# One guard over two columns becomes two guards over one, and a column total moves back in TensorE's order

## The chip, the cores and the metric

One NeuronCore of a Trainium2 chip runs the kernel as one program. The metric is the device time of an execution in microseconds; the time of a kernel is the median of its runs.

## What is computed

An attention layer with pooled keys is followed by two feed-forward layers. For 12288 tokens of 128 channels:

```python
kv_pool = kv.reshape(B, H // r, r, W // r, r, C).mean(axis=(2, 4))   # r = 4, 768 keys
k = v = kv_pool.reshape(B, -1, C) @ w_sr
s = (1.0 / np.sqrt(C)) * (q @ k.transpose(0, 2, 1))
a = np.exp(s - s.max(-1, keepdims=True))
a /= a.sum(-1, keepdims=True) + 1e-09
x = a @ v
h = x @ w_in                                       # 128 -> 2048
x = (np.maximum(h, 0) + alpha * np.minimum(h, 0)) @ w_out
h = x @ w_in2
x = (h * (1.0 / (1.0 + np.exp(-1.702 * h)))) @ w_out2
```

## The kernel before

The tokens go in 24 blocks `j` of 512 columns; channels lie on the 128 partitions. Every float32 operand of a large product is split into a high and a low float16 part, and a product is three matmuls (L443, L444, L445: high by high, low by high, high by low), which are 128x512 each. A block has four tiles of scores (`S`, L692 to L696), six products with the values (`V`), and 16 products in each of the four layers `L1` to `L4`.

Before a split the operand is scaled by a power of two, so that it fits float16. The scale comes from a bound on the largest absolute value. VectorE takes the maximum of each partition (`top`, L612, L764, L766) into `ta`; the **guard**, a `tensor_scalar` with max (it has the line of the helper `ts`, L408), lifts it to at least 2^-60 and writes it as bfloat16 to `td`; TensorE adds up the partitions with a matrix of ones, the **total** (`total`, name `scmm`, L622); VectorE takes the exponent out of the sum (`scp`) and turns it into the factor (`scc`). Then ScalarE writes the high part (L640) and VectorE the low one (L642). Three operands of a block are scaled so: `q`, `x` (the attention's output) and `y` (the output of the first feed-forward layer).

`x_prep(j)` for `j` from 3 to 21 does x of block `j` and q of block `j + 2` together: two maxima stand in the two columns of `ta2`, one guard over both columns writes `td2`, one total has two columns. `scale_of` is the way of all the others, with one column; it has the guard from block 3 on (`j > 2`).

A total, and every product of `L1` and `L3`, writes one of the three PSUM banks of `pool_h` (in the profile two of them are `hb` and one is `bk`). ScalarE and VectorE empty a bank: L830 (relu) and L832 (prelu) behind `L1`, L871 (tanh) and L873 (gelu) behind `L3`. The float16 parts of the hidden layers are made by ScalarE (L808) and, by a subtraction, mostly by GpSimd (L811).

The order of the instructions of each engine is worked out when the program is built. `op` records an operation with its engine, the time for which it keeps the engine, its duration, what it reads and writes, and a priority. `Plan.order` then places them one by one: the first 725 by the hand-made list `ORDER`, all later ones by taking for each engine what can start first in the plan, and among equals the lowest priority. An operation may start when what it reads has ended, plus a latency from `LAT` (54 ns from VectorE to TensorE); an entry of the read list may carry a third member, an offset that is taken off that time. TensorE is one queue in order: what waits at its head holds up everything behind it.

Of the kernel before, what the change touches and what calls it, by code (L numbers as in the profile page):

```python
# [17 lines left out]
ALU = mybir.AluOpType  # L18
# [98 lines left out]
class Plan:  # L117
# [5 lines left out]
    def op(self, eng, occ, dur, fn, r=(), w=(), prio=0.0, gate=None, name="", lock=False, dma=False):  # L123
        o = Op()
        o.eng, o.occ, o.dur, o.fn, o.gate, o.name, o.lock, o.dma = eng, occ, dur, fn, gate, name, lock or eng == "POOL", dma or eng == "SP"
        o.keys = [k for k in (self.tag, name.split(",")[0] if name.startswith(LAYER) else name) if k]
        o.prio = prio + sum(SHIFT.get(k, 0) for k in o.keys)
        k = f"{self.tag}|{name}"
        self.seen[k] = self.seen.get(k, -1) + 1
        o.uid = f"{k}|{self.seen[k]}"  # L130
        o.warm = 0
        o.n, o.succs, o.start, o.end = len(self.ops), [], None, None
        preds = {}

        def need(p, off):
            if p is not o:
                preds[p] = min(preds.get(p, off), off)

        bufs = []
        for x in r:  # L140
            b, part, off = (x + (0,))[:3] if isinstance(x, tuple) else (x, None, 0)
            if part not in b.writers:
                raise RuntimeError(f"{name} reads {b.name} {part} before it is written")
            for p in b.writers[part]:
                need(p, off)
            b.readers.setdefault(part, []).append(o)
            bufs.append(b)
        for x in w:
            b, part = x[:2] if isinstance(x, tuple) else (x, None)
            for p in b.readers.get(part, ()):  # L150
                need(p, 0)
            for p in b.writers.get(part, ()):
                need(p, 0)
            if (b, part) not in [(y[0], y[1]) if isinstance(y, tuple) else (y, None) for y in r]:
                b.readers[part] = []
            b.writers[part] = [o]
            bufs.append(b)
        o.bufs = list(dict.fromkeys(bufs + [b.also for b in bufs if b.also]))
        for b in o.bufs:
            b.ops.append(o)  # L160
        if gate is not None:
            preds.setdefault(gate, None)
        o.preds = list(preds.items())
        self.ops.append(o)
        return o
# [202 lines left out]
def dve(ns, n):  # L368
    return int(ns - 1.04 * (TB - n))
# [14 lines left out]
def record(nc, T):  # L384

    pl = Plan()
    op = pl.op
# [6 lines left out]
    def cols(ap, j):  # L394
        return ap[:, 0:SZ[j]]
# [7 lines left out]
    def fixed(name):  # L403
        return Buf(None, name)

    def ts(out, in0, s1, op0, s2=None, op1=None):
        if op1 is None:
            return V.tensor_scalar(out=out, in0=in0, scalar1=s1, scalar2=None, op0=op0)  # L408
        else:
            return V.tensor_scalar(out=out, in0=in0, scalar1=s1, scalar2=s2, op0=op0, op1=op1)  # L410

    def small(fn, r, w, prio, gate=None, occ=66, dur=150, name="small", lock=False):
        return op("DVE", occ, dur, fn, r, w, prio, gate, name, lock)
# [6 lines left out]
    pool_h = Pool([Slot(None, [cell[2]]), Slot(None, [cell[3]]), Slot(single[0], [cell[4]])])  # L420
# [15 lines left out]
    def new(name):  # L436
        return rings[name].buf(name)

    B = {name: fixed(name) for name in ("ident", "ones", "wsr", "al", "oma", "k_hi", "k_lo", "v_hi", "v_lo", "vsc", "vun", "kq",
                                        "kx", "kxc", "ky", "kyc", "kk", "vm", "wh", "wl", "am", "aov", "warm")}  # L440
# [169 lines left out]
    def top_of(j, x, xb, psum, prio, gate):  # L610
        d = new("td" if j < 3 else "ta")
        op("DVE", dve(608 if psum else 593, SZ[j]), dve(692, SZ[j]), lambda: V.tensor_reduce(out=d.ap, in_=x(), axis=AX.X, op=ALU.max,  # L612
                                                                     apply_absolute_value=True), [xb], [d], prio, gate, name="top")
        return d

    def total(pool, cols_, least, prio, n=1):

        pm = pool.buf("pt")

        def f():  # L620
            for i, (c, _) in enumerate(cols_):
                mm(out=pm.ap[:, 0:n], lhsT=T["ones"], rhs=c(), start=i == 0, stop=least is None and i == len(cols_) - 1)  # L622
            if least is not None:
                mm(out=pm.ap[:, 0:n], lhsT=T["ones"], rhs=least, start=False, stop=True)
        op("PE", 45 * len(cols_) + (45 if least is not None else 0), 0, f, [b for _, b in cols_] + [B["ones"]], [pm], prio, name="scmm")
        return pm

    def scale_of(d, pool, kc, kcb, prio, j=0):
        if j > 2:
            a, d = d, new("td")  # L630
            small(lambda: ts(d.ap, a.ap, 2.0 ** -60, ALU.max), [a], [d], prio)
        pm = total(pool, [(lambda: d.ap, d)], None if j > 2 else T["least"], prio)
        p, c = new("scp"), new("scc")
        small(lambda: ts(p.ap, pm.ap[:, 0:1].bitcast(I32), 0x7F800000, ALU.bitwise_and), [pm], [p], prio, occ=117)
        small(lambda: ts(c.ap, p.ap, -1.0, ALU.mult, kc(), ALU.add), [p] + kcb, [c], prio + .01, occ=110, dur=200)
        return c, p

    def parts(j, hi, lo, x, xb, c, prio, gate=None, psum=True):
        n = SZ[j]
        op("ACT", act(569 if psum else 613, n), act(700 if psum else 742, n), lambda: A.activation(cols(hi.ap, j), x(), AF.Copy, scale=c.ap.bitcast(F32)),  # L640
           [xb, c], [hi], prio, gate, name="hi")
        op("DVE", dve(665, n), dve(750, n), lambda: V.scalar_tensor_tensor(out=cols(lo.ap, j), in0=x(), scalar=c.ap.bitcast(F32), in1=cols(hi.ap, j),  # L642
                                                           op0=ALU.mult, op1=ALU.subtract), [xb, c, hi], [lo], prio + .01, gate, name="lo", lock=not psum)
# [115 lines left out]
    def x_prep(j, prio):  # L759
        x = xacc[j]  # L760
        pl.tag = f"X{j}"
        if 2 < j < NB - 2:
            t, a, d, p2, c, qc_ = q_t[j + 2], new("ta2"), new("td2"), new("scp2"), new("scc"), new("qcc")
            op("DVE", dve(593, TB), dve(692, TB), lambda: V.tensor_reduce(out=a.ap[:, 1:2], in_=t.ap, axis=AX.X, op=ALU.max, apply_absolute_value=True),  # L764
               [t], [(a, 1)], prio, name="top")
            op("DVE", dve(608, TB), dve(692, TB), lambda: V.tensor_reduce(out=a.ap[:, 0:1], in_=x.ap, axis=AX.X, op=ALU.max, apply_absolute_value=True),  # L766
               [x], [(a, 0)], prio, name="top")
            small(lambda: ts(d.ap, a.ap, 2.0 ** -60, ALU.max), [(a, 0), (a, 1)], [d], prio + .01)
            pm = total(pool_h, [(lambda: d.ap, d)], None, prio + .1, 2)
            small(lambda: ts(p2.ap, pm.ap[:, 0:2].bitcast(I32), 0x7F800000, ALU.bitwise_and), [pm], [p2], prio + .1, occ=117)  # L770
            p, q = Half(p2, 0), Half(p2, 1)
            small(lambda: ts(c.ap, p.ap, -1.0, ALU.mult, T["kxc"], ALU.add), [p2, B["kxc"]], [c], prio + .11, occ=110, dur=200)
            small(lambda: ts(qc_.ap, q.ap, -1.0, ALU.mult, QC, ALU.add), [p2], [qc_], prio + .12)
            qc[j + 2] = qc_, q
        else:
            d = top_of(j, lambda: cols(x.ap, j), x, True, prio, None)
            c, p = scale_of(d, pool_h, lambda: T["kxc"], [B["kxc"]], prio + .1, j)
        xh[j], xl[j] = new("xh"), new("xl")
        parts(j, xh[j], xl[j], lambda: cols(x.ap, j), x, c, prio + .2)
        xsc[j] = p  # L780
        pl.tag = ""
# [111 lines left out]

    q_prep(0, -660)
    vp = total(pool_x, [(lambda i=i: T["vm"][:, i:i + 1], (B["vm"], i)) for i in range(3)], T["least_v"], -650)
    small(lambda: ts(T["vun"], vp.ap[:, 0:1].bitcast(I32), 0x7F800000, ALU.bitwise_and), [vp], [B["vun"]], -647, occ=117)
    small(lambda: ts(T["vsc"], T["vun"], -1.0, ALU.mult, float(268 << 23), ALU.add), [B["vun"]], [B["vsc"]], -646)
# [30 lines left out]
    for t in range(SZ[0] // P):  # L928
        att_v(0, t, PR["v0"] + PR["a0s"] * t, None)
    x_prep(0, PR["x0"])  # L930

    for n, x in enumerate(LOADS):
# [183 lines left out]
```

## Time and profile before

| | us |
|---|---|
| median of 3 runs | 1259.17 |
| lowest and highest | 1256.1, 1259.45 |
| the profiled execution | 1257.87 |
| its span, first to last instruction | 1255.8 |
| TensorE busy in the span | 1215.5 |
| a block in the steady part, from total to total (1017.59 to 1067.77) | 50.18 |

The profile is of one execution. A matmul is shown with a duration of 0.38 us, but the next one of the same engine starts earlier; the rate at which TensorE works is read from the distance of the starts. The granted clock of TensorE is full throughout (1.000 in the mean).

### The profile page before, as it was taken

What the parts mean: (1) busy time and instruction counts of PE and PEld (TensorE: products, weight loads), DVE (VectorE), ACT (ScalarE), POOL (GpSimd) and SP (SyncE); (2) the same over time, 40 slices, a digit from 0 to 9 for tenths busy, and PEclk for the clock granted to TensorE, in tenths of its full rate; (3) what the DMA queues carried; (4) which work ended last, traced back from release to release, by engine and by line L of the source; (5) the groups of instructions that cost most, each with busy time, mean ns of one, the idle gap of its engine ahead of it and who ended that gap; (6) DMA issues with size and microseconds to landing.
All of it is one profiled execution on the core that took longest, in us unless ns stands there. A gap on an engine that the chain in (4) does not pass through costs nothing.

```text
span 1255.8 us, 18308 instructions
## 1 busy us (share of the span) xinstructions
PE 1215.5 (97%) x5829; PEld 569.3 (45%) x5832; DVE 1005.0 (80%) x1821; ACT 1099.7 (88%) x1939; POOL 804.8 (64%) x688
## 2 busy tenths in 40 slices
PE   5699999999999999999999999999999999999998
PEld 4344444444444444444444444444444444444443
DVE  5999998887877877878778778787787787876756
ACT  1899888888989989889899898898998988988888
POOL 1577566666657666666576666665766766667764
PEclk9999999999999999999999999999999999999999
DMA  9932222222121123121211221212111212120000
GB/s 372 215 62 48 44 43 47 53 37 46 35 55 35 36 45 55 34 47 34 56 34 38 43 55 34 46 36 55 34 40 41 55 34 47 34 47 13 9 10 17
DMA packets 165377, 66.67 MB, mean 53 GB/s; under 512 B 156448, under 2 KB 156576, under 8 KB 164256
## 3 DMA queue, kind: packets, MB, share of 16 engines
q1 hardware_dynamic: 164992, 65.43, 23.4%
q8 instruction: 45, 0.74, 0.2%
q14 instruction: 52, 0.43, 0.1%
q10 hardware_dynamic: 288, 0.07, 0.0%
HBM read 21.05 MB, written 6.29 MB: 22 GB/s over the span
## 4 chain that ended last, share of the span: by engine, by line
PE 60%; DVE 3%; ACT 1%; issue 0%; DMA 0%; POOLq 0%; POOL 0%; SPq 0%; ACTq 0%
PE bk L445 12%; PE bk L444 12%; PE bk L443 12%; PE hb L443 6%; PE hb L444 6%; PE hb L445 6%; PE sa L692 1%; PE sa L693 1%; PE sa L696 1%; DVE td L408 1%; DVE arena L832 1%; DVE ta L766 1%; ACT arena L808 0%; DMA q<-in_q 0%; PE hb L622 0%
## 5 line engine op out<-in xcount | busy, mean ns | idle before, releaser
L811 POOL TENSOR_TENSOR arena<-arena 128x512 f16<-128x512 f32 x656 | 769.0, 1191 | 403.4 <-ACT arena L808 286.9
L808 ACT CAST arena<-arena 128x512 f16<-128x512 f32 x740 | 449.5, 631 | 64.4 <-DVE arena L832 27.1
L873 DVE SCALAR_TENSOR_TENSOR arena<-arena,hb 128x512 f32<-128x512 f32 x261 | 178.8, 685 | 57.6 <-ACT arena L871 55.2
L832 DVE SCALAR_TENSOR_TENSOR arena<-arena,oma,hb 128x512 f32<-128x512 f32 x262 | 194.4, 743 | 29.9 <-ACT arena L830 26.3
L871 ACT ACTIVATE arena<-hb,yu 128x512 f32<-128x512 f32 x261 | 183.1, 702 | 12.8 <-PE hb L445 11.2
L830 ACT ACTIVATE arena<-hb 128x512 f32<-128x512 f32 x262 | 160.3, 613 | 23.1 <-PE hb L445 18.3
L445 PE MATMUL bk<-arena,w2h 128*128 128x512 f16 x384 | 145.6, 379 | 0.7 <-POOL arena L811 0.7
L445 PE MATMUL bk<-arena,w4h 128*128 128x512 f16 x384 | 145.6, 379 | 0.2 <-POOL arena L811 0.2
L444 PE MATMUL bk<-arena,w4l 128*128 128x512 f16 x384 | 145.6, 379 | 0.0
L443 PE MATMUL bk<-arena,w4h 128*128 128x512 f16 x384 | 145.6, 379 | 0.0
L444 PE MATMUL bk<-arena,w2l 128*128 128x512 f16 x384 | 145.6, 379 | 0.0
L443 PE MATMUL bk<-arena,w2h 128*128 128x512 f16 x384 | 145.6, 379 | 0.0
L873 DVE SCALAR_TENSOR_TENSOR arena<-arena,bk 128x512 f32<-128x512 f32 x123 | 84.1, 683 | 37.4 <-ACT arena L871 37.1
L731 DVE SCALAR_TENSOR_TENSOR alo<-sa,r,ah 128x768 f16<-128x768 f32 x88 | 89.5, 1017 | 18.1 <-ACT ah L716 13.0
L832 DVE SCALAR_TENSOR_TENSOR arena<-arena,oma,bk 128x512 f32<-128x512 f32 x122 | 90.7, 744 | 12.6 <-ACT arena L830 10.0
L443 PE MATMUL hb<-xh,w1h 128*128 128x512 f16 x262 | 99.2, 379 | 1.2 <-ACT xh L640 0.9
L443 PE MATMUL hb<-yh,w3h 128*128 128x512 f16 x261 | 98.9, 379 | 0.8 <-DVE arena L873 0.8
L445 PE MATMUL hb<-xl,w1h 128*128 128x512 f16 x262 | 99.3, 379 | 0.2 <-DVE xl L642 0.2
L444 PE MATMUL hb<-xh,w1l 128*128 128x512 f16 x262 | 99.3, 379 | 0.0
L445 PE MATMUL hb<-yl,w3h 128*128 128x512 f16 x261 | 98.9, 379 | 0.0
L444 PE MATMUL hb<-yh,w3l 128*128 128x512 f16 x261 | 98.9, 379 | 0.0
L871 ACT ACTIVATE arena<-bk,yu 128x512 f32<-128x512 f32 x123 | 85.3, 693 | 12.2 <-PE bk L445 10.6
(159 smaller groups left out, 2102.8 us busy)
## 6 DMA issues: line engine op xcount, KB each, us to landing
q<-in_q SPq DMA_DIRECT2D x24, 256.0 KB, 3.0
arena<-in_kv SPq DMA_DIRECT2D x12, 512.0 KB, 10.0
out<-arena SPq DMA_DIRECT2D x24, 256.0 KB, 2.0
raw<-in_moe_w_in SPq DMA_DIRECT2D x4, 1024.0 KB, 13.8
raw<-in_moe_w_out SPq DMA_DIRECT2D x4, 1024.0 KB, 12.0
eh<-ah SPq DMA_TRANSPOSE x96, 2.8
el<-alo SPq DMA_TRANSPOSE x96, 2.8
wsr<-in_w_sr ACTq DMA_DIRECT2D x1, 64.0 KB, 2.8
```

The source lines that it names most:

```text
L408: return V.tensor_scalar(out=out, in0=in0, scalar1=s1, scalar2=None, op0=op0)
L443: mm(out=o, lhsT=wh, rhs=xh, start=start, stop=False)
L444: mm(out=o, lhsT=wl, rhs=xh, start=False, stop=False)
L445: mm(out=o, lhsT=wh, rhs=xl, start=False, stop=stop)
L692: mm(out=s.ap[:, h, 0:HALF], lhsT=qh[j].ap[:, ts_], rhs=T["k_hi"][:, hs], start=True, stop=False)
L731: op("DVE", 933, 1019, lambda: V.scalar_tensor_tensor(out=al.ap, in0=dst(), scalar=r.ap, in1=ah.ap, op0=ALU.mult, op1=ALU.subtract), [e, r ...
L808: op("ACT", act(508, n), act(618, n), lambda: A.copy(cols(hi.ap, j), cols(g.ap, j)), [g], [hi], s + 1.2, name=f"{nm}h{j},{m}")
L811: lambda: (V if on else G).tensor_tensor(out=cols(lo.ap, j), in0=cols(g.ap, j), in1=cols(hi.ap, j), op=ALU.subtract),
L830: op("ACT", act(488, n), act(597, n), lambda: A.activation(cols(g.ap, j), cols(h.ap, j), AF.Relu, scale=-1.0), [h], [g], s + .3, name=f"re ...
L832: op("DVE", dve(658, n), dve(746, n), lambda: V.scalar_tensor_tensor(out=cols(g.ap, j), in0=cols(g.ap, j), scalar=T["oma"][:, m:m + 1], in ...
L871: op("ACT", act(581, n), act(687, n), lambda: A.activation(cols(g.ap, j), cols(h.ap, j), AF.Tanh, scale=u.ap[:, 0:1]), [h, u], [g], s + .3 ...
L873: op("DVE", dve(605, n), dve(687, n), lambda: V.scalar_tensor_tensor(out=cols(g.ap, j), in0=cols(g.ap, j), scalar=1.0, in1=cols(h.ap, j), ...
```

## The change

`total` takes a list `need` of what it waits for. In `x_prep` for blocks 3 to 21 the one guard over two columns is written as two guards over one column each, the q column first; each waits for its own maximum alone. The total waits for both, with an offset of -300, which adds 300 ns to the time at which the planner lets it start. `scale_of` gives its total the same offset from block 3 on. No wait on the chip is added by the offset: it is used by the planner alone. The list `ORDER` stays; the numbers that it holds go up to 899, and the operations of `x_prep(3)` have numbers from 928 on. By the description of the change, from block 4 on other products stand between a guard and its total.

```diff
-    def total(pool, cols_, least, prio, n=1):
+    def total(pool, cols_, least, prio, n=1, need=None):
...
-        op("PE", 45 * len(cols_) + (45 if least is not None else 0), 0, f, [b for _, b in cols_] + [B["ones"]], [pm], prio, name="scmm")
+        op("PE", 45 * len(cols_) + (45 if least is not None else 0), 0, f, (need or [b for _, b in cols_]) + [B["ones"]], [pm], prio, name="scmm")
...
-        pm = total(pool, [(lambda: d.ap, d)], None if j > 2 else T["least"], prio)
+        pm = total(pool, [(lambda: d.ap, d)], None if j > 2 else T["least"], prio, 1, [(d, None, -300 if j > 2 else 0)])
...
-            small(lambda: ts(d.ap, a.ap, 2.0 ** -60, ALU.max), [(a, 0), (a, 1)], [d], prio + .01)
-            pm = total(pool_h, [(lambda: d.ap, d)], None, prio + .1, 2)
+            for k in (1, 0):
+                small(lambda k=k: ts(d.ap[:, k:k + 1], a.ap[:, k:k + 1], 2.0 ** -60, ALU.max), [(a, k)], [(d, k)], prio + .01)
+            pm = total(pool_h, [(lambda: d.ap, d)], None, prio + .1, 2, [(d, 0, -300), (d, 1, -300)])
```

## Rows read from the trace of the kernel before

**Rows 1.** The page, part 1: busy time, share of the span and instructions.

```profile
PE 1215.5 (97%) x5829; PEld 569.3 (45%) x5832; DVE 1005.0 (80%) x1821; ACT 1099.7 (88%) x1939; POOL 804.8 (64%) x688
```

**Rows 2.** Waits of PE: who waited for whom, us, times, longest.

```profile
PE hb L622 <- DVE td L408: 8.6, 17, 0.5
...
PE bk L622 <- DVE td L408: 1.0, 3, 0.5
```

**Rows 3.** Groups of VectorE by shape: busy us, mean ns, idle before.

```profile
L408 DVE TENSOR_SCALAR td<-ta 128x2 bf16<-128x2 f32 x19 | 19.6, 1032 | 0.0
...
L408 DVE TENSOR_SCALAR td<-ta 128x1 bf16<-128x1 f32 x25 | 3.7, 149 | 0.0
```

**Rows 4.** In order of time, VectorE's guard and GpSimd: start, us, operation.

```profile
1016.43 1.10 DVE L408 TENSOR_SCALAR td<-ta 128x2 bf16<-128x2 f32 x1
...
1016.36 1.16 POOL L811 TENSOR_TENSOR arena<-arena 128x512 f16<-128x512 f32 x1 [0.71 <-ACT arena L808]
```

**Rows 5.** The same around the guard of a y.

```profile
1084.02 0.15 DVE L408 TENSOR_SCALAR td<-ta 128x1 bf16<-128x1 f32 x1
1084.08 0.95 DVE L702 TENSOR_REDUCE nm<-sa 128x1 f32<-128x768 f32 x1
...
1083.38 2.27 POOL L811 TENSOR_TENSOR arena<-arena 128x512 f16<-128x512 f32 x2 [0.27 <-ACT arena L808]
```

**Rows 6.** In order of time, TensorE up to the total of an x.

```profile
1016.48 0.38 PE L444 MATMUL bk<-arena,w2l 128*128 128x512 f16 x1
1016.70 0.38 PE L445 MATMUL bk<-arena,w2h 128*128 128x512 f16 x1
1017.59 0.16 PE L622 MATMUL hb<-td,ones 128*128 128x2 bf16 x1 [0.51 <-DVE td L408]
```

**Rows 7.** In order of time, a bank emptied by VectorE and written next.

```profile
1026.29 0.69 DVE L873 SCALAR_TENSOR_TENSOR arena<-arena,hb 128x512 f32<-128x512 f32 x1
...
1027.03 0.38 PE L443 MATMUL hb<-xh,w1h 128*128 128x512 f16 x1
```

**Rows 8.** In order of time, VectorE's maximum of the q column.

```profile
1004.06 0.69 DVE L764 TENSOR_REDUCE ta<-q 128x1 f32<-128x512 f32 x1 [1.39 <-DMA q<-in_q]
```

**Rows 9.** In order of time, the totals of the x of block 3 and the y of block 3.

```profile
170.08 0.16 PE L622 MATMUL bk<-td,ones 128*128 128x2 bf16 x1 [0.28 <-DVE td L408]
...
231.80 0.16 PE L622 MATMUL bk<-td,ones 128*128 128x1 bf16 x1 [0.25 <-DVE td L408]
```

**Rows 10.** In order of time, TensorE: first and last total of a y.

```profile
281.34 0.16 PE L622 MATMUL bk<-td,ones 128*128 128x1 bf16 x1
...
1083.81 0.38 PE L445 MATMUL bk<-arena,w4h 128*128 128x512 f16 x1
1084.22 0.16 PE L622 MATMUL bk<-td,ones 128*128 128x1 bf16 x1
```

**Rows 11.** In order of time, behind the total of an x: VectorE, ScalarE, TensorE.

```profile
1017.79 0.16 DVE L408 TENSOR_SCALAR scp<-hb 128x2 int32<-128x2 int32 x1 [0.26 <-PE hb L622]
...
1018.47 0.21 DVE L410 TENSOR_SCALAR scc<-scp,kxc 128x1 int32<-128x1 int32 x1
...
1016.47 0.69 ACT L871 ACTIVATE arena<-bk,yu 128x512 f32<-128x512 f32 x1 [0.24 <-PE bk L445]
...
1018.52 0.60 ACT L830 ACTIVATE arena<-hb 128x512 f32<-128x512 f32 x1 [0.86 <-PE hb L445]
1019.02 0.68 ACT L640 ACTIVATE xh<-bk,scc 128x512 f16<-128x512 f32 x1
...
1023.77 0.38 PE L443 MATMUL hb<-xh,w1h 128*128 128x512 f16 x1
```

**Rows 12.** In order of time, behind the total of a y: VectorE, TensorE.

```profile
1085.60 0.15 DVE L408 TENSOR_SCALAR scp<-bk 128x1 int32<-128x1 int32 x1
...
1086.84 0.38 PE L443 MATMUL bk<-yh,w3h 128*128 128x512 f16 x1
```

**Rows 13.** Busy time of each engine in one stretch: us, PE, PEld, DVE, ACT, POOL.

```profile
1025.00:1030.00 5.00, 5.00 (x25) 2.24 (x23) 3.98 (x6) 5.00 (x11) 3.54 (x3) 1.00 0.55 111
```

## The prediction

> **What bounds the kernel now.** I read the page first. TensorE is busy 1215.5 of 1255.8 us; no other engine passes 88% [rows 1]. TensorE's work doesn't change, so only time in which it waits can be won, and the next view is what it waited for. Two lines of that list name `td`, the output of the guard, as what the total (L622) waited for: 17 times on `hb`, 8.6 us, and 3 times on `bk`, 1.0 us [rows 2]. The view by shape then tells the two guards apart: over one column 149 ns in the mean of 25, over two columns 1032 ns in the mean of 19 [rows 3]. The guard does next to no arithmetic in either, so its length had to be looked for in the order of time.
>
> There, in one block of the steady part, the two-column guard starts at 1016.43 and lasts 1.10 us, to 1017.53. GpSimd's subtraction (L811) runs from 1016.36 to 1017.52 [rows 4]. The guard ends when GpSimd's instruction ends. A one-column guard at 1084.02 took 0.15 us although two GpSimd instructions ran back to back from 1083.38 to 1085.65 [rows 5]. So two columns wait for GpSimd here and one column doesn't.
>
> What this costs TensorE: the last matmul of a product starts at 1016.70, the total at 1017.59 [rows 6]. A product's matmuls start 0.22 us apart (1016.48, 1016.70), so the total stands 0.89 - 0.22 = 0.67 us late. The view shows 0.51 as idle, because it counts from a modelled end (0.38 us after the start); each wait is therefore worth 0.16 us more than the view says. Behind the total, TensorE's whole queue stands.
>
> **The change part by part.**
>
> *The guard over two columns becomes two over one column* (blocks 3 to 21, 19 times). Removed: 19 x 1032 ns; added: 38 x 149 ns [rows 3], on VectorE. The guard of the q column needs only the q maximum, which is there some 11 us earlier (L764 at 1004.06), so it leaves the chain [rows 8]. The guard of the x column starts at 1016.43 as now and ends at 1016.58; TensorE is free for the total at 1016.70 + 0.22 = 1016.92. The total's operand is then 0.34 us early instead of 0.67 late, wherever the total stands. The sum: 17 waits show 8.6 us, plus 17 x 0.16 = 2.7, gives 11.3 us [rows 2]; one more two-column guard, block 3's, held a total at 170.08 for 0.28 + 0.16 = 0.44 us [rows 9]. Together 11.7 us. The added instruction is hidden: VectorE begins the next operation 0.06 us after a one-column guard's start (1084.02, then 1084.08) [rows 5], and it sat idle 1.39 us just before L764 [rows 8]. Without this cover it would be 19 x 0.15 = 2.9 us at the most on VectorE, against 19 x 0.88 = 17 us that VectorE gets back.
>
> [...]
>
> *The total is planned 300 ns later* (`need`, and the same for the one-column guards of `scale_of` from block 3 on). The planner takes for each engine the work that can start first. Put with the times of the trace: an x guard ending at 1016.58, plus the 54 ns that the kernel's list `LAT` has from VectorE to TensorE, plus 300, gives 1016.93, just past the boundary at 1016.92, so one product of three matmuls, 0.65 us, goes ahead of the total, and behind the total nothing is added. For x this is worth nothing more: the wait is gone already. For y it is: the one-column guard at 1084.02 ends at 1084.17, 0.05 us before its total at 1084.22, which stands 1084.22 - 1083.81 - 0.22 = 0.19 us late. There are 17 such totals from 281.34 to 1084.22, taken at 0.2 us each [rows 10], and one of 0.25 + 0.16 = 0.41 us at 231.80 [rows 9]: 17 x 0.2 + 0.41 = 3.8 us. With a product of 0.65 us between, the total has 0.46 us in hand and the wait goes.
>
> *What the later total delays.* Its result goes to VectorE (scp 1017.79, scc 1018.47), ScalarE (L640, 1019.02 to 1019.70) and VectorE for the low part; the first product that reads them starts at 1023.77 [rows 11]. That is 4.1 us behind L640, and only the product's third matmul reads the low part; 0.65 us fit in. For y the reader (scp) starts at 1085.60, 1.4 us after the total [rows 12], so 0.65 us fit before it too.
>
> *What is late next.* Each of the three `hb`/`bk` banks must be emptied by ScalarE and VectorE before TensorE writes it again. The tightest is at 1027.03, 0.05 us after VectorE's L873 ends at 1026.98 [rows 7]. It lies in a stretch in which ScalarE is busy 5.00 of 5.00 us [rows 13]. So TensorE keeps its 0.67 us only if that stretch starts as much earlier. Ahead of it ScalarE sat idle 0.86 us, until 1018.52, for the very product behind the total (`hb` L445) [rows 11]. That product will end at 1017.57 - it now stands in front of the total - so ScalarE's L830 starts near 1017.83, 0.69 earlier. ScalarE's next, L640, needs scc: the total goes at 1017.57, and VectorE, free since 1016.6, has meanwhile done the L873 whose input was ready at 1017.16 (L871 from 1016.47 for 0.69 us) [rows 11]; scp follows at 1017.8 and scc at 1018.0, before ScalarE is free at 1018.3. The stretch moves as a whole, and so I take the full gain.
>
> Sum: 11.7 + 3.8 = 15.5 us. The profiled execution took 1257.87 us, its span 1255.8 and 2.07 around it; it becomes 1242.4. The median of the runs shown is 1259.17, 1.3 above the profiled one; the same 15.5 us make it **1243.7 us**. No stall outside these totals is touched, among them those before 100 us and at the end.
>
> **The rivals.**
>
> *ScalarE's full stretch keeps its start.* If scp still runs first and scc still starts at 1018.47 (the total is at 1017.57 where it was at 1017.59), L640 can start at 1018.7, only 0.31 us earlier than now, and the banks come free 0.67 - 0.31 = 0.36 us too late in each of 18 blocks: 6.5 us come back, 1250.2 us. For it speaks the 0.05 us of slack; against it, that L873 can run ahead of scp.
>
> *One column waits for GpSimd too.* The guard of x then ends at 1017.53 as now. The total, one product later, then starts at 1017.6, hardly later than TensorE is free, but scp and scc aren't earlier: the same 1250.2 us. Against it stand the 25 guards of 149 ns [rows 3]. [...]
>
> *The order doesn't move.* The boundary is passed by only 0.01 us above; if the planner leaves the totals in their place, the change does half of what it says. The x term stays, the y term goes: 1259.17 - 11.7 = 1247.5 us.
>
> *Something else stands at the same place*, so that TensorE loses there what it won: within 0.3%, near 1258 us.
>
> *Slower: the total holds a bank longer.* It occupies one of three banks from its matmul until scp has read it, now 1084.22 to 1085.75; the product that writes `bk` next (1086.84) has 1.09 us in hand [rows 10, 12]. If in the new order scp is queued behind a further maximum (L702) and two L873, 0.95 + 2 x 0.69 = 2.33 us [rows 5, 7], the bank is 1.24 us late in 18 blocks: 22.3 us against 15.5, 1266 us. It decides from scp 1.09 + 0.87 = 1.96 us later on. Nothing in the edit adds work between total and scp.
>
> **How the numbers follow.** Chances: forecast 0.66; ScalarE's stretch 0.16; one column waits 0.05; order unmoved 0.05; lost again 0.04; slower 0.04. The range takes in all cases but the last two: down to 1240.5 (the fastest run before, 1256.1, less 15.5), up to 1252 (1250.2 and half the spread of 3.4 us of the runs before). About 0.3%, 3.8 us, is what a measurement of this kernel can tell from no change: faster 0.92, same 0.04, slower 0.04.
>
> **What would show it.** In the profile after: no group of `td` from two columns, and 63 guards of 0.15 us; L622's waits for `td` down from 9.6 us to under 1.5 us; a product with a start between each guard's end and its total; a block's period of 50.18 us down to some 49.3. The step on ScalarE is wrong if small waits of L443 on `hb` for VectorE's L832 or L873 appear some 10 us behind each x total. The forecast is wrong if `td` guards last a microsecond still, or if the block's period stays above 49.8 us.

## The result, and the profile after

The changed kernel takes 1243.71 us (median, 1242.8 to 1244.79) against 1257.98 us for the kernel before, run beside it (1256.1 to 1259.45): a ratio of 0.9888, with a 95% interval of 0.9873 to 0.9902, which is a saving between 12.3 and 16.0 us. The medians lie 14.3 us apart. The forecast was 1243.7 us, from a saving of 15.5 us on a median of 1259.17. The saving was 1.2 us too large, inside the interval, and the median of the three runs of before that it was taken from lies 1.2 us above that of all five. The two errors cancel: that the forecast time is right to a tenth of a microsecond is luck. The profiled execution took 1242.8 us, its span 1241.0.

From here on the lines of `kernel.py` beyond the edit have moved by one: L811 is L812, L830 is L831, L873 is L874.

The page, part 1, and the waits of TensorE for what the guards write (us, times, longest), which answer to [rows 1, 2]; then VectorE's groups by shape (busy us, mean ns, idle before), for [rows 3]:

```profile
PE 1212.1 (98%) x5832; PEld 569.5 (46%) x5832; DVE 991.4 (80%) x1840; ACT 1098.4 (89%) x1939; POOL 804.2 (65%) x688
...
PE hb L622 <- DVE td L612: 0.8, 1, 0.8
...
PE bk L622 <- DVE td L408: 0.5, 1, 0.5
...
L408 DVE TENSOR_SCALAR td<-ta 128x1 bf16<-128x1 f32 x63 | 9.4, 149 | 0.0
```

The group of two columns is gone; 63 guards of 149 ns stand in place of 44. VectorE is busy 13.6 us less. The 20 waits for a guard of [rows 2] have become one of 0.5 us, at 86.12 in the hand-made part of the order, which stands in the kernel before too, and a new one of 0.8 us for a maximum (L612), of which more below.

In order of time, around the total of an x, first VectorE, then GpSimd, TensorE and ScalarE (start, us, operation):

```profile
1003.31 0.15 DVE L408 TENSOR_SCALAR td<-ta 128x1 bf16<-128x1 f32 x1
1004.06 0.69 DVE L874 SCALAR_TENSOR_TENSOR arena<-arena,bk 128x512 f32<-128x512 f32 x1 [0.60 <-ACT arena L872]
1004.67 0.16 DVE L408 TENSOR_SCALAR scp<-hb 128x2 int32<-128x2 int32 x1
1004.87 0.21 DVE L410 TENSOR_SCALAR scc<-scp,kxc 128x1 int32<-128x1 int32 x1
...
1003.23 1.16 POOL L812 TENSOR_TENSOR arena<-arena 128x512 f16<-128x512 f32 x1 [0.71 <-ACT arena L809]
...
1003.57 0.38 PE L445 MATMUL bk<-arena,w2h 128*128 128x512 f16 x1
1003.79 0.38 PE L443 MATMUL hb<-xh,w1h 128*128 128x512 f16 x1
...
1004.22 0.38 PE L445 MATMUL hb<-xl,w1h 128*128 128x512 f16 x1
1004.44 0.17 PE L622 MATMUL hb<-td,ones 128*128 128x2 bf16 x1
...
1004.70 0.60 ACT L831 ACTIVATE arena<-hb 128x512 f32<-128x512 f32 x1 [0.16 <-PE hb L622]
1005.19 0.68 ACT L640 ACTIVATE xh<-bk,scc 128x512 f16<-128x512 f32 x1
```

The guard starts 0.08 us behind the start of GpSimd's instruction (0.07 in [rows 4]), and is over after 0.15 us instead of 1.10. The added guard, that of q, starts at 992.08, and VectorE's next operation 0.06 us later. In the kernel before, the product of `hb<-xh,w1h` stood behind the total of [rows 6]:

```profile
1017.62 0.38 PE L443 MATMUL hb<-xh,w1h 128*128 128x512 f16 x1
```

It now starts 0.22 us after the last matmul ahead of it, and the total 0.22 us after that product's last: TensorE loses nothing. Set against the start of the guard, scc starts 1.56 us later instead of 2.04, and ScalarE's L640 1.88 instead of 2.59 [rows 4, 11].

Around the total of a y:

```profile
1020.02 0.15 DVE L408 TENSOR_SCALAR td<-ta 128x1 bf16<-128x1 f32 x1
...
1021.60 0.15 DVE L408 TENSOR_SCALAR scp<-hb 128x1 int32<-128x1 int32 x1
...
1019.80 0.38 PE L445 MATMUL bk<-arena,w4h 128*128 128x512 f16 x1
1020.01 0.38 PE L443 MATMUL hb<-yh,w3h 128*128 128x512 f16 x1
...
1020.45 0.38 PE L445 MATMUL hb<-yl,w3h 128*128 128x512 f16 x1
1020.66 0.17 PE L622 MATMUL hb<-td,ones 128*128 128x1 bf16 x1
```

One product stands between, the 0.2 us of [rows 10] are gone, and scp follows 0.94 us after the total. One period of the steady part, busy time of each engine (us, PE, PEld, DVE, ACT, POOL):

```profile
1004.44:1053.79 49.35, 49.35 (x238) 22.93 (x237) 39.41 (x73) 45.29 (x82) 32.91 (x28) 1.00 0.23 44
```

TensorE is busy 49.35 of 49.35 us; the period was 50.18.

### The profile page after: what moved, and what is told of

The parts are those of the page before. It is cut to its first block, busy times and chain, and to the rows that moved or that the text cites. A ratio compares the mean times of both kernels' runs of the same rounds, so it can differ in the third digit from the quotient of the medians.

```text
span 1241.0 us, 18323 instructions
## 1 busy us (share of the span) xinstructions
PE 1212.1 (98%) x5832; PEld 569.5 (46%) x5832; DVE 991.4 (80%) x1840; ACT 1098.4 (89%) x1939; POOL 804.2 (65%) x688
## 5 line engine op out<-in xcount | busy, mean ns | idle before, releaser
L812 POOL TENSOR_TENSOR arena<-arena 128x512 f16<-128x512 f32 x656 | 768.4, 1190 | 390.4 <-ACT arena L809 311.4
L874 DVE SCALAR_TENSOR_TENSOR arena<-arena,hb 128x512 f32<-128x512 f32 x254 | 173.4, 684 | 70.1 <-ACT arena L872 68.7
L833 DVE SCALAR_TENSOR_TENSOR arena<-arena,oma,hb 128x512 f32<-128x512 f32 x257 | 190.5, 742 | 25.6 <-ACT arena L831 21.1
L872 ACT ACTIVATE arena<-hb,yu 128x512 f32<-128x512 f32 x254 | 177.3, 699 | 13.3 <-PE hb L445 10.7
L831 ACT ACTIVATE arena<-hb 128x512 f32<-128x512 f32 x257 | 156.4, 610 | 9.3 <-PE hb L445 3.9
L443 PE MATMUL bk<-arena,w4h 128*128 128x512 f16 x384 | 145.5, 379 | 0.0
L443 PE MATMUL bk<-arena,w2h 128*128 128x512 f16 x384 | 145.4, 379 | 0.0
L874 DVE SCALAR_TENSOR_TENSOR arena<-arena,bk 128x512 f32<-128x512 f32 x130 | 88.9, 684 | 38.0 <-ACT arena L872 37.0
L833 DVE SCALAR_TENSOR_TENSOR arena<-arena,oma,bk 128x512 f32<-128x512 f32 x127 | 94.3, 743 | 11.9 <-ACT arena L831 9.5
L443 PE MATMUL hb<-xh,w1h 128*128 128x512 f16 x257 | 97.4, 379 | 1.1 <-ACT xh L640 0.6
L443 PE MATMUL hb<-yh,w3h 128*128 128x512 f16 x254 | 96.2, 379 | 1.1 <-DVE arena L874 0.8
L872 ACT ACTIVATE arena<-bk,yu 128x512 f32<-128x512 f32 x130 | 90.8, 698 | 6.8 <-PE bk L445 5.3
L445 PE MATMUL hb<-yl,w3h 128*128 128x512 f16 x254 | 96.2, 379 | 0.0
L444 PE MATMUL hb<-yh,w3l 128*128 128x512 f16 x254 | 96.2, 379 | 0.0
## 6 DMA issues: line engine op xcount, KB each, us to landing
raw<-in_moe_w_out SPq DMA_DIRECT2D x4, 1024.0 KB, 12.3
```

The source lines that it names most:

```text
L443: mm(out=o, lhsT=wh, rhs=xh, start=start, stop=False)
L444: mm(out=o, lhsT=wl, rhs=xh, start=False, stop=False)
L445: mm(out=o, lhsT=wh, rhs=xl, start=False, stop=stop)
L812: lambda: (V if on else G).tensor_tensor(out=cols(lo.ap, j), in0=cols(g.ap, j), in1=cols(hi.ap, j), op=ALU.subtract),
L831: op("ACT", act(488, n), act(597, n), lambda: A.activation(cols(g.ap, j), cols(h.ap, j), AF.Relu, scale=-1.0), [h], [g], s + .3, name=f"re ...
L833: op("DVE", dve(658, n), dve(746, n), lambda: V.scalar_tensor_tensor(out=cols(g.ap, j), in0=cols(g.ap, j), scalar=T["oma"][:, m:m + 1], in ...
```

## The experiments

Times are medians; a saving is against the kernel before, run beside it on the same chip (1257.40 us for the first four rows, 1257.54 on another chip for the others). The period is the distance of two x totals in the steady part of each trace.

| kernel | us | ratio to before, 95% interval | saving, us | period, us |
|---|---|---|---|---|
| guards split, order kept | 1245.18 | 0.9906 (0.9889 to 0.9922) | 12.2 | 49.51 |
| order alone | 1245.75 | 0.9906 (0.9891 to 0.9920) | 11.7 | 49.44 |
| both, order from block 4 | 1241.63 | 0.9876 (0.9861 to 0.9890) | 15.8 | 49.35 |
| the changed kernel again | 1243.68 | 0.9893 (0.9878 to 0.9908) | 13.7 | 49.35 |
| guards split, order of y alone | 1243.01 | 0.9885 (0.9871 to 0.9898) | 14.5 | 49.38 |
| offset 1500 | 1245.56 | 0.9905 (0.9890 to 0.9921) | 12.0 | 49.45 |
| y guards two wide | 1266.01 | 1.0067 (1.0054 to 1.0080) | -8.5 | 50.58 |
| three columns (one run) | 1258.18 | | -0.6 | 50.18 |

The changed kernel, run again, was expected to be 14 to 15.5 us faster; it was 13.7.

**The guards split, the order kept.** The offsets are taken out of the changed kernel:

```diff
-            pm = total(pool_h, [(lambda: d.ap, d)], None, prio + .1, 2, [(d, 0, -300), (d, 1, -300)])
+            pm = total(pool_h, [(lambda: d.ap, d)], None, prio + .1, 2, [(d, 0), (d, 1)])
...
-        pm = total(pool, [(lambda: d.ap, d)], None if j > 2 else T["least"], prio, 1, [(d, None, -300 if j > 2 else 0)])
+        pm = total(pool, [(lambda: d.ap, d)], None if j > 2 else T["least"], prio, 1)
```

> The two one-column guards of the change, but no offset of 300 ns: the plan puts every total where it stands in the kernel before. Theory (the wait is the two-column guard's, for GpSimd): the waits of the x totals go (17 x 0.67 + 0.44 = 11.7 us) and those of the y totals, 0.2 us each, stay: 11.7 us faster than before, 1246.3 against a before of 1258.0. Rival (the new order does it): within 2 us of before.

It saved 12.2 us, where 11.7 were expected. The period fell by 0.67 us, to the hundredth what a late x total cost, and the 0.2 us of the y totals stayed. The rival falls: TensorE's instructions stand in the order of the kernel before.

**The order alone.** The guard over two columns stays, and its total gets the offset; the total of `scale_of` keeps the offset of the changed kernel:

```diff
-            for k in (1, 0):
-                small(lambda k=k: ts(d.ap[:, k:k + 1], a.ap[:, k:k + 1], 2.0 ** -60, ALU.max), [(a, k)], [(d, k)], prio + .01)
-            pm = total(pool_h, [(lambda: d.ap, d)], None, prio + .1, 2, [(d, 0, -300), (d, 1, -300)])
+            small(lambda: ts(d.ap, a.ap, 2.0 ** -60, ALU.max), [(a, 0), (a, 1)], [d], prio + .01)
+            pm = total(pool_h, [(lambda: d.ap, d)], None, prio + .1, 2, [(d, None, -300)])
```

> The offset of 300 ns alone: totals stand one product later, and the guard over two columns stays. The guards must still last about 1.03 us in the mean. Theory: TensorE works through the product in the meantime and hardly waits for the total (under 0.1 us in a block), the y waits go too, but scp and scc come no earlier, so ScalarE's full stretch starts only some 0.3 us earlier and 0.36 us of the 0.67 come back as bank waits: 15.5 - 6.5 = 9 us faster, near 1249. Rival A (the order alone is worth all of it): within 1 us of the changed kernel, 14 to 15.5 us faster. Rival B (what counts is the length of the guard): under 5 us faster.

It saved 11.7 us, between the theory's 9 and rival A's 14, and far more than rival B's 5; none of the three was right. VectorE's groups by shape, then in order of time VectorE, TensorE and ScalarE at one x (lines as in the kernel before):

```profile
L408 DVE TENSOR_SCALAR td<-ta 128x2 bf16<-128x2 f32 x19 | 19.5, 1024 | 0.0
...
956.06 1.10 DVE L408 TENSOR_SCALAR td<-ta 128x2 bf16<-128x2 f32 x1
957.08 0.68 DVE L873 SCALAR_TENSOR_TENSOR arena<-arena,hb 128x512 f32<-128x512 f32 x1
957.67 0.15 DVE L408 TENSOR_SCALAR scp<-hb 128x2 int32<-128x2 int32 x1
...
956.97 0.38 PE L445 MATMUL bk<-xl,w1h 128*128 128x512 f16 x1
957.22 0.16 PE L622 MATMUL hb<-td,ones 128*128 128x2 bf16 x1
...
958.11 0.69 ACT L640 ACTIVATE xh<-bk,scc 128x512 f16<-128x512 f32 x1
```

The guard is as long as ever, and the total waits only 0.03 us, since a product fills the time. scp stands behind L873 here too, and L640 starts 2.05 us after the guard's start: 0.54 earlier than before, where the theory allowed 0.31, and 0.17 later than in the changed kernel. What comes back is 49.44 - 49.35 = 0.09 us in a block, not 0.36. So the two parts are very nearly alternatives: alone they save 12.2 and 11.7 us, together 13.7.

**The order from block 4 on.**

```diff
-        pm = total(pool, [(lambda: d.ap, d)], None if j > 2 else T["least"], prio, 1, [(d, None, -300 if j > 2 else 0)])
+        pm = total(pool, [(lambda: d.ap, d)], None if j > 2 else T["least"], prio, 1, [(d, None, -300 if j > 3 else 0)])
...
-            pm = total(pool_h, [(lambda: d.ap, d)], None, prio + .1, 2, [(d, 0, -300), (d, 1, -300)])
+            pm = total(pool_h, [(lambda: d.ap, d)], None, prio + .1, 2, [(d, 0, -300 if j > 3 else 0), (d, 1, -300 if j > 3 else 0)])
```

> The whole change, but the offset only from block 4 on, so that the plan up to the x of block 3 is that of the kernel before. In the changed kernel the total of the y of block 2 waits 1.0 us at 179.8 and a product at 235.5 waits 0.5, where before they waited 0 and 0.1. Theory (block 3's total, moved, reorders the stretch behind it): both go, 1.0 to 1.4 us faster than the changed kernel run beside it. Rival (those waits come from elsewhere): the same time as the changed kernel within 0.3 us, and the waits stay.

It is the fastest: 1241.63 us (1241.17 to 1243.13), 2.05 us under the changed kernel beside it (1243.23 to 1245.75), more than the 1.0 to 1.4 expected. Both waits are gone from its trace, and a third, of 0.3 us at 865.15, of which more below. Where the larger one came from is seen in order of time in three traces. The kernel before, VectorE and GpSimd:

```profile
177.02 0.75 DVE L642 SCALAR_TENSOR_TENSOR ql<-q,qcc,qh 128x512 f16<-128x512 f32 x1
...
175.45 1.16 POOL L811 TENSOR_TENSOR arena<-arena 128x512 f16<-128x512 f32 x1 [1.00 <-ACT arena L808]
177.06 5.07 POOL L811 TENSOR_TENSOR arena<-arena 128x512 f16<-128x512 f32 x4 [0.45 <-ACT arena L808]
```

The changed kernel, VectorE, TensorE and GpSimd:

```profile
177.43 1.74 DVE L642 SCALAR_TENSOR_TENSOR ql<-q,qcc,qh 128x512 f16<-128x512 f32 x1
...
179.09 0.68 DVE L612 TENSOR_REDUCE td<-bk 128x1 bf16<-128x512 f32 x1
...
179.83 0.16 PE L622 MATMUL hb<-td,ones 128*128 128x1 bf16 x1 [0.83 <-DVE td L612]
...
173.92 7.38 POOL L812 TENSOR_TENSOR arena<-arena 128x512 f16<-128x512 f32 x6 [1.01 <-ACT arena L809]
```

The kernel with the order from block 4:

```profile
175.21 0.74 DVE L642 SCALAR_TENSOR_TENSOR ql<-q,qcc,qh 128x512 f16<-128x512 f32 x1
...
177.58 0.69 DVE L612 TENSOR_REDUCE td<-bk 128x1 bf16<-128x512 f32 x1
...
175.26 7.31 POOL L812 TENSOR_TENSOR arena<-arena 128x512 f16<-128x512 f32 x6 [0.46 <-ACT arena L809]
```

In the changed kernel block 3's moved total shifts what the planner does next, so that the subtraction for q (L642) starts in the middle of six GpSimd instructions in a row and takes 1.74 us. In the other two it starts 0.04 and 0.05 us before GpSimd goes on, and takes 0.75 and 0.74. The maximum behind it, which feeds the total of the y of block 2, is late, and TensorE waits 0.83 + 0.16 = 1.0 us. That the order is the cause is shown by the third kernel. That it is the moved total of x, and not that of y, is shown by two more traces: the wait for L612 stands in that of the order alone (0.91 us shown as idle, at 180.49), and not in that of the next experiment, in which the x totals keep their place. That L642 was held by GpSimd is read from the rows and was not tried by itself.

**The guards split, the order of y alone.** The x total's offset is taken out, that of `scale_of` stays:

```diff
-            pm = total(pool_h, [(lambda: d.ap, d)], None, prio + .1, 2, [(d, 0, -300), (d, 1, -300)])
+            pm = total(pool_h, [(lambda: d.ap, d)], None, prio + .1, 2, [(d, 0), (d, 1)])
```

> One-column guards, and the offset only in scale_of, so that the totals of y stand one product later and those of x where they stood before. Theory: the x waits are gone by the guards alone, the y waits by the order: 15 us faster than before, the changed kernel's time within 1.5 us. Rival (the moved x totals carry a part): more than 3 us slower than the changed kernel.

1243.01 us, with a saving of 14.5 against 13.7 for the changed kernel, which ran on another chip, and a period of 49.38 against 49.35. The rival falls. With short guards the moved x total is worth 0.03 us in a block, and the y order 49.51 - 49.38 = 0.13.

**An offset of 1500.** Each -300 becomes -1500.

> The change with an offset of 1500 ns in place of 300: an x total then stands behind a product and a tile of scores more than before, some 1.6 us behind its time before; a y total behind three products. Theory (4.1 us in hand behind L640, 1.4 us between a y total and its reader): no wait of TensorE for the low or high part of x, the changed kernel's time within 3 us. Rival (a later total holds its bank longer and pushes the scale chain): each x total costs up to 1 us, 10 us or more slower than the changed kernel.

1245.56 us: it saves 1.7 us less than the changed kernel, which ran on another chip, where the theory allowed 3 and the rival asked for 10. In order of time, VectorE's low part of an x and the first product that reads it; then a bank emptied by VectorE and TensorE at it, behind the total of a y:

```profile
1009.69 0.74 DVE L642 SCALAR_TENSOR_TENSOR xl<-bk,scc,xh 128x512 f16<-128x512 f32 x1
...
1011.19 0.38 PE L443 MATMUL hb<-xh,w1h 128*128 128x512 f16 x1
...
1024.57 0.69 DVE L874 SCALAR_TENSOR_TENSOR arena<-arena,bk 128x512 f32<-128x512 f32 x1
...
1023.17 0.17 PE L622 MATMUL hb<-td,ones 128*128 128x1 bf16 x1
...
1024.92 0.38 PE L445 MATMUL hb<-yl,w3h 128*128 128x512 f16 x1
1025.32 0.38 PE L443 MATMUL bk<-xh,w1h 128*128 128x512 f16 x1
```

The low part is still done 0.76 us before its product starts. What is lost stands elsewhere: at 1025.32 the step is 0.40 instead of 0.22 us, just behind the end of L874 at 1025.26, which gives the bank free. This wait of 0.18 us stands at the same place in 16 blocks running, and the period is 49.45. So later totals do cost something at a bank, but 0.1 us in a block and not the rival's 1. The bank that is late is not the total's own (`hb` at 1023.17) but `bk`; by what path the later totals delay it is not shown.

**The y guards two wide.** In the kernel before, the tiles of `scale_of`'s guard are two columns wide instead of one; the second column of `ta` is set to zero at the start, and the total leaves it out.

```diff
-        pm = total(pool, [(lambda: d.ap, d)], None if j > 2 else T["least"], prio)
+        pm = total(pool, [(lambda: d.ap[:, 0:1], d)], None if j > 2 else T["least"], prio)
...
-        op("DVE", dve(608 if psum else 593, SZ[j]), dve(692, SZ[j]), lambda: V.tensor_reduce(out=d.ap, in_=x(), axis=AX.X, op=ALU.max,
+        o = lambda: d.ap[:, 0:1]
+        op("DVE", dve(608 if psum else 593, SZ[j]), dve(692, SZ[j]), lambda: V.tensor_reduce(out=o(), in_=x(), axis=AX.X, op=ALU.max,
```

> The kernel before, with the guard of scale_of (y, from block 3 on) written over two columns instead of one; the second column is zero and isn't used by the total. Nothing else is changed. Theory (an operation over two columns waits for GpSimd's running instruction, one over one column doesn't): the y guards, 0.15 us now, become 0.3 to 1.6 us long wherever GpSimd works, their totals wait 0.4 us or more on top of 0.2: 17 x 0.4 = 7 us slower than before or more. Rival (the length of the x guard has to do with the place, not with the width): the y guards stay under 0.2 us and the time is that of before within 1 us.

8.5 us slower. VectorE, GpSimd and TensorE around one y, in order of time (lines moved by three):

```profile
1039.08 0.55 DVE L408 TENSOR_SCALAR td<-ta 128x2 bf16<-128x2 f32 x1
...
1038.44 2.27 POOL L814 TENSOR_TENSOR arena<-arena 128x512 f16<-128x512 f32 x2 [0.28 <-ACT arena L811]
...
1038.86 0.38 PE L445 MATMUL bk<-arena,w4h 128*128 128x512 f16 x1
1039.68 0.16 PE L625 MATMUL bk<-td,ones 128*128 128x1 bf16 x1 [0.44 <-DVE td L408]
```

The same guard in the same place, which took 0.15 us one column wide, takes 0.55 us and ends at 1039.63, where the first of the two GpSimd instructions ends (shown alone it lasts 1.16 us, to 1039.60). The total is 0.82 - 0.22 = 0.60 us late instead of 0.2: the 0.40 us by which the period grew. The wait goes with the width, not with the place.

Nor is it the width alone that takes the time. In the same trace one y's guard falls into a pause of GpSimd, from 230.36 to 231.47; VectorE, then GpSimd:

```profile
230.65 0.17 DVE L408 TENSOR_SCALAR td<-ta 128x2 bf16<-128x2 f32 x1
...
227.58 2.78 POOL L814 TENSOR_TENSOR arena<-arena 128x512 f16<-128x512 f32 x2
231.47 1.16 POOL L814 TENSOR_TENSOR arena<-arena 128x512 f16<-128x512 f32 x1 [1.10 <-ACT arena L811]
```

It takes 0.17 us. Two columns are slow here only beside GpSimd's work.

**Three columns.** In the kernel before, `ta2` and `td2` are three columns wide instead of two; the third is set to zero at the start, and the total leaves it out.

```diff
-            pm = total(pool_h, [(lambda: d.ap, d)], None, prio + .1, 2)
+            pm = total(pool_h, [(lambda: d.ap[:, 0:2], d)], None, prio + .1, 2)
```

> The kernel before, with the x guard over three columns; the third is zero and isn't used by the total. One look at the guard's length. If an odd count of three takes the same way as two, the mean stays near 1.03 us and the time that of before; if only even counts wait for GpSimd, the guards last 0.15 us and the x waits are gone as with two single columns, some 11.7 us faster.

VectorE's groups by shape:

```profile
L408 DVE TENSOR_SCALAR td<-ta 128x3 bf16<-128x3 f32 x19 | 19.4, 1021 | 0.0
L408 DVE TENSOR_SCALAR td<-ta 128x1 bf16<-128x1 f32 x25 | 3.7, 149 | 0.0
```

Three columns wait like two. The single run took 1258.18 us, inside the spread of the kernel before beside it (1256.45 to 1259.21).

## Why the prediction was right, and where it was off

*The guard.* Its cause was read rightly: the two-column guard waits for GpSimd's running instruction, a one-column one doesn't. The wide y guards, long beside GpSimd and short in its pause, and the split alone show it; in the kernel before, each of the 19 two-column guards ends within 0.03 us of the end of a GpSimd instruction. The price of an x total, 0.67 us (0.51 shown as idle, and 0.16), was exact (period 50.18 to 49.51). In the changed kernel no x total waits.

*The chain behind the total.* Put on the times of the guard, the prediction had scp at 1.4 us after the guard's start, scc at 1.6 and L640 at 1.9. Measured are 1.36, 1.56 and 1.88, with L874 ahead of scp as argued. ScalarE's full stretch moved as a whole, so the first rival didn't come about, save in one block (at 865.15, below). Where it was tried by itself, in the order alone, the price was 0.09 us in a block, not 0.36: its premise, that scp still runs ahead of L873, was wrong there too.

*The order.* One product came between guard and total, for x and for y, and the 0.2 us at the y totals went. But the y order is worth 0.13 us in a block (49.51 - 49.38), not 0.2. In its place L443 waits 0.04 and 0.05 us, 4.6 and 8.5 us behind each moved y total (at 827.57 and 831.50 behind the one at 822.98), for banks that VectorE's L833 and L874 have just emptied. These two waits stand in the traces of the kernels that move the y totals by 300, and not in that of the guards split with the order kept. "For x this is worth nothing more" holds: 0.03 us in a block. But the prediction credited the x term to the guard alone and didn't say that the order by itself would have brought nearly the same. It priced long guards with the new order at 1250.2, a saving of 9.0 us; measured were 11.7.

*The sum.* 15.5 us were forecast. From the product at 145.36 in the kernel before (143.83 after) to the late matmul at 1251.21 (1236.39 after) the changed kernel is 1105.85 - 1092.56 = 13.3 us shorter in the profiled executions; the rest of the difference of the spans, 1.5 us, lies before that. There the start varies in one kernel too: that product starts at 143.83 and at 144.49 in the two profiled executions of the changed kernel. Of the missing 2.2 us, 1.0 is the new wait at 179.83, 0.4 a wait at 235.48 that grew from 0.12 to 0.50, 0.3 a single one at 865.15; and 17 x 0.04 = 0.7 lies in the period, 49.35 instead of 49.31 (the y order 0.07 short, less the 0.03 of the moved x totals); where the 0.2 us come from by which these are more than 2.2 is open. Two steps failed. The larger is the sentence that no stall outside these totals is touched: moving block 3's total made the planner lay out anew what follows it, which cost 1.4 us at 179.83 and 235.48. The other is the size of the y term, 0.2 us a block where 0.13 was measured. With the order kept until block 4 the same stretch is 1234.76 - 143.90 = 1090.86, 15.0 us shorter than before. The wait at 865.15 is the sign that the prediction had named, in one block alone. ScalarE, then TensorE:

```profile
856.64 0.60 ACT L831 ACTIVATE arena<-hb 128x512 f32<-128x512 f32 x1 [0.44 <-PE hb L622]
...
864.66 0.38 PE L445 MATMUL bk<-arena,w4h 128*128 128x512 f16 x1
865.15 0.38 PE L443 MATMUL hb<-xh,w1h 128*128 128x512 f16 x1
```

It stands 9 us behind the x total at 856.10, on `hb`, where VectorE's L874 ends at 865.10. ScalarE's L831 had sat idle for 0.44 us in this block instead of 0.16, so that its full stretch began 0.28 us late. The other profiled execution of the changed kernel has it in the same block; the kernel with the order from block 4 does not. Why it is this block is not shown. One slip of the prediction changes nothing: 1256.1 less 15.5, the low end of its range, is 1240.6 and not 1240.5.

## What to carry to other kernels

When a tiny operation lasts a microsecond, look in the order of time at what ends with it on another engine; here the cure was to make it narrower, at the price of one more instruction of 0.06 us. A wait at the head of an in-order queue can be shortened or filled with other work, and either alone brought most of the gain, so the price of one part must be taken with the other both present and absent. After an edit to a planner's times, look for new waits where the plan goes from a hand-made to a computed order.

## What the runs showed of the hardware

A `tensor_scalar` from SBUF to SBUF, float32 to bfloat16, lasts 149 ns in the mean of 63 with one column, 1024 and 1032 in the mean of 19 with two and 1021 with three, among GpSimd subtractions of 1.19 us. Where no GpSimd instruction ran, two columns took 0.17 us.

The Trainium skill, "VectorE: DVE Perf Modes", section "What auto-detection actually checks", has VectorE take a mode with two ports for one source in SBUF where the outermost non-unit counts of source and destination are both even, or equal. The runs agree with it for two and for three columns if this mode is what makes them wait, which no run shows. With one column there is no count other than one, and there the guard didn't wait.
